# One of four VectorE softmax patterns made by an accumulating DMA, with 560 instead of 504 score tiles on VectorE

## The chip, the core and the metric

The kernel runs on one core of one Trainium2 chip. The metric is device time in microseconds (us); the kernel before has a median of 757.29 us in three runs. Engines are named as the profile names them: PE is TensorE (matrix products; PEld its weight loads), ACT is ScalarE, DVE is VectorE, POOL is GpSimd, SP is the engine that issues most DMAs.

## The reference, cut to what matters

```
x = A_x                                   # 2048 tokens x 512, 32 heads of 16
g = sigmoid((x * gate_w).sum(-1))         # a gate for each token
qkv = x @ A_wqkv
p = softmax(q @ k.T * 16 ** -0.5)         # per head, 2048 x 2048 scores
a = (p @ v) @ A_wo
# branch B: linear attention over the same x
phi_q = [softmax(q' @ w_phi), softmax(-q' @ w_phi)], phi_k likewise
b = (phi_q @ (phi_k.T @ v') / den) @ B_wo
return g * a + (1 - g) * b
```

Nearly all the work is the softmax attention of branch A: 32 heads with 2048 x 2048 scores each, every one of which has to go through an exponential.

## The kernel before, in words

**Tiles.** A unit is a score tile of 128 keys x 512 queries of one head. There are 2048 of them, in 512 rows ("packs") of four heads; sixteen rows make a group g (all keys of four heads against one chunk of 512 queries), so there are 32 groups. Scores are computed transposed (keys on partitions), on one of four strips of 32 rows of the PE array (`_scores`, L1040). The product with the values (`_values`, L1147) runs on one of four strips of 32 columns and adds up in a PSUM bank that stays open for the group. A column of ones in the values gives the denominator, and `_norm` divides at the group's end.

**Two ways to an exponential.** Most units go to ACT, two at a time: `_exp` (L1088) reads 128 x 1024 scores from PSUM and writes bf16 into `ET`, a ring of `NSLOT` = 22 tiles. The exponential of tile a waits for the value product of tile a - `NSLOT`. The units in `away` go to DVE: `NUMS` says how many in each of the 32 groups, 504 in all. DVE makes the exponential out of bits. `v_bits` (L946) scales a score and adds an origin, rounds to a 16-bit whole number, and those bits are read as a bf16 number, a piecewise linear 2^x. To smooth the error, four such patterns are made, with the bits shifted by 0, 31, 64 and 95; the last two are multiplied with values scaled by `RATIO` (`V2`), and all four products add up in the same accumulator (`pvx`).

**A batch** (`_vector_batch`) is four such units. Before, DVE writes the first pattern into the first half of a tile `va` (two buffers), one step instruction (L971) makes the second pattern beside it (2048 elements, + 31), and one step of 4096 elements makes patterns three and four from both in a tile `vs` (two buffers, + 64). So all four patterns are in memory side by side, and each has its own four matmuls.

**The order of the work** is written out by a planner (`Plan`) when the program is built. Every instruction is an `Op` with an engine, an assumed cost, a priority (roughly the row at which it is due) and the Ops that it depends on. `order` repeatedly takes the Op that could start earliest by these costs; among those ready it goes by `rank`. `now` is the row of the latest scores. An Op with `urgent` at or below `now` goes ahead. `shift` adds a pseudo-random offset to the priorities, drawn from `SEEDS`, once ahead of the ordering. The result is a fixed queue for each engine; `emit` puts a semaphore wait where an Op needs another engine's result. An engine carries out its queue strictly in this order, POOL and SP with their DMA issues among them. `o.port` marks POOL's instructions and some of DVE's, the steps among them, which the planner doesn't lay over one another.

**PSUM** has eight banks: four (`NRING`) hold scores for ACT, the others serve the accumulators, DVE's scores, the projections and branch B. **Fills:** where PE would have little to do, the planner puts matmuls with zeros into the open accumulator (`_fill`, L1154).

**Other lines that matter here.** Projections of q, k and v (L711, L827), the masks of q on POOL (L803), values scaled for `V2` on POOL (L844), the transposition of an accumulator on DVE (L1168), its normalisation on DVE and POOL (L1176 to L1185) and the small DMAs that regroup it (L1191). Branch B's maxima, sums and reciprocals run on DVE and POOL, its exponentials on ACT (L1335, 16 of them). `LEAD` = 7 says how many rows ahead of its first unit a batch's scores are due, `QDUE` = 20 how many rows ahead a q projection is, and `URGENT` = 4 how many rows after its own a value product becomes urgent.

Of the kernel before, what the change touches and what calls it, by code (L numbers as in the profile page):

```python
# [7 lines left out]
ALU = mybir.AluOpType  # L8
AX = mybir.AxisListType

P = 128
# [28 lines left out]
class Op:  # L40
    def __init__(self, eng, fn, cost, name, prio, rel, kind, lat):
# [21 lines left out]
        self.group = None  # L63


class Plan:
# [11 lines left out]
    def __init__(self):  # L78
# [11 lines left out]
        self.todo = {}  # L90

# [18 lines left out]
    def op(self, eng, fn, cost, reads=(), writes=(), deps=(), name="", prio=0.0, rel=-99, kind="full",  # L110
# [23 lines left out]
        o.port = eng == "POOL" or eng == "DVE" and name in self.PORT  # L134
# [5 lines left out]
    SEEDS = (3340, 7601, 0, 849, 2310, 7659, 5600, 4117, 3297, 4434, 5571, 2308, 3491, 696, 0, 2037, 1043, 4583, 3197, 9690, 0, 1465, 7801, 8165, 7230, 6142, 5708, 481, 3824, 4801, 1237, 3959, 2876, 7231)  # L140

    def shift(self):
        count = {}
        for o in self.ops:
            k = count[o.name] = count.get(o.name, 0) + 1
            s = self.SEEDS[min(max(int(o.prio // 16), 0), 33)] if o.prio >= 0 else 0
            if s:
                h = sum(map(ord, o.name)) * 7919 + k * 104729 + s * 65537
                h = (h ^ h >> 13) * 2654435761 & 0xFFFFFFFF
                o.prio += (s % 3 + 1) * (((h ^ h >> 16) & 1023) / 511.5 - 1)  # L150
# [64 lines left out]
    def order(self):  # L215
        avail = {e: [] for e in self.ENGS}
        for o in self.ops:
            o.left = len(o.deps)
            for d in o.deps:
                d.users.append(o)  # L220
# [9 lines left out]
        while left:  # L230
            best = None
# [94 lines left out]
    def emit(self, nc, ctx):  # L326
# [6 lines left out]
        count = dict.fromkeys(self.ENGS, 0)  # L333
        for e, q in self.queues.items():
            for o in q:
                if o.name.startswith("dma"):
                    o.sem = (ctx.enter_context(nc.semaphore(o.name)), 16 * len(o.fn) if isinstance(o.fn, list) else 16)
# [70 lines left out]
class _Kernel:  # L408
    NRING = 4
    GROUPS = (2, 2)  # L410
    NSLOT = 22
# [4 lines left out]
    NA, NST, LEAD = 2, 2, 7  # L416
# [21 lines left out]
    ALONE, EARLY = 12, 10  # L438
    PVP = 10
# [18 lines left out]
    def build(self):  # L458
        with ExitStack() as ctx:
# [10 lines left out]
            p.shift()  # L470
# [4 lines left out]
    def _memory(self, ctx):  # L475
# [67 lines left out]
        tiles = [sb(f"vs{k}", [P, 2, self.PACK, QCH], U16) for k in range(self.NST + self.NA)]  # L543
        self.vs, self.va = tiles[:self.NST], tiles[self.NST:]
# [341 lines left out]
    NUMS = (6, 10, 16, 14, 14, 16, 16, 19, 13, 19, 17, 12, 17, 11, 19, 19, 14, 20, 12, 16, 19, 13, 17, 16, 15, 20, 12, 20, 17, 21, 21, 13)  # L886

    def _plan_vector(self):
# [13 lines left out]
        self.hooks = {}  # L902
# [17 lines left out]
    def _vector_batch(self, number, units, due):  # L920
# [10 lines left out]
        for j, u in enumerate(units):  # L931
# [16 lines left out]
            if j < 2 * pairs and j % 2:  # L948
# [4 lines left out]
                def two(e, j=j, jobs=twin[j // 2]):  # L953
                    lo, hi = sorted(x.bank for x in jobs)
                    return bits(e, va[:, 0, j - 1:j + 1, :], self.ps[:, lo:hi + 1:hi - lo, :])
                parts.append(op("DVE", two, self.c_dve(1024), deps=[first[0], m] + war, name="v_bits", prio=first[2],
                                release=first[1], also=job))
            else:
                parts.append(op("DVE", lambda e, j=j, job=job: bits(e, va[:, 0, j, :], self._bank(job)),
# [4 lines left out]
        slot = self.n_step % self.NST  # L964
        self.n_step += 1
        vs, b_vs, b_vb = self.vs[slot], self.b_vs[slot], self.b_vb[number % self.NA]
        for k in range(4):
            tile, buf = (vs if k > 1 else va)[:, k % 2], b_vs if k > 1 else b_vb if k else b_va
            if k in (1, 2):
                src, dst = (va[:, 0, 0:n], va[:, 1, 0:n]) if k == 1 else (va[:, :, 0:n], vs[:, :, 0:n])  # L970
                o = op("DVE", lambda e, k=k, src=src, dst=dst: e.tensor_scalar(dst, src, float(STEPS[k - 1]), None,  # L971
                                                                               op0=ALU.add),
                       0.16 + k * n * QCH * 0.00026, reads=[b_va] + [b_vb] * (k - 1), writes=[buf], name="v_step",
                       prio=units[0] / 4 - 4)
# [724 lines left out]
```

## Time and profile before

| what | us |
|---|---|
| runs, median (lowest to highest of 3) | 757.29 (757.25 to 759.3) |
| span of the profiled execution, first to last instruction | 755.8 |
| PE busy | 744.3 |
| DVE busy | 719.9 |
| ACT busy | 741.1 |
| POOL busy | 228.6 |

The profiled execution's own time is given only as its span; the runs' median lies 1.5 us above it. "Busy" is the time in which at least one instruction's record is open. On this core records of one engine overlap: the next instruction starts before the record of the one before has ended. So the pace of an unbroken run (start to start) is shorter than the mean length of a record, and both are used below. A line of a group reads: source line, engine, operation, out<-in, sizes, count, then busy us and mean ns of one, then the idle time of the engine just before these instructions and whom it waited for. A line of the timeline reads: start, length, engine, line, operation, count, and in brackets the idle time before it.

### The profile page before, as it was taken

The page shows a single profiled execution, that of the slowest core. Times are in us where ns is not written, and L with a number is a line of the kernel's source. Part 1 is how long each engine was busy: PE and PEld are TensorE (multiplying, and loading weights), DVE is VectorE, ACT ScalarE, POOL GpSimd, SP SyncE. Part 2 cuts the span into 40 slices and gives each one's busy share as a digit, 9 for nine tenths or more (in the row PEclk, how much of TensorE's full clock was granted, in tenths as well). Part 3 has the DMA queues.
Part 4 walks back from the last instruction along what each step waited for, and adds up shares of the span by engine and source line. Part 5 has one row for each costly group of instructions (what it writes and reads, how often), then busy time and mean ns, then how long its engine had stood idle before and what let it go on. Part 6 is the DMA issues. An engine that isn't in the chain of part 4 may idle for free.

```text
span 755.8 us, 17204 instructions
## 1 busy us (share of the span) xinstructions
PE 744.3 (98%) x7246; PEld 219.7 (29%) x7246; DVE 719.9 (95%) x1128; ACT 741.1 (98%) x796; POOL 228.6 (30%) x317
## 2 busy tenths in 40 slices
PE   8999999999999999999999999999999999999998
PEld 3323222323332222222232323222232222223222
DVE  4788999999999999999999999999999999999997
ACT  6999999999999999999999999999999999999996
POOL 2213206241534334234407051431615051260010
PEclk9999999999999999999999999999999999999999
DMA  9610000001001000000200312112022103111010
GB/s 220 144 24 6 9 8 6 12 2 15 2 2 15 1 8 10 6 11 3 42 15 19 40 24 48 30 34 39 8 47 33 29 23 44 22 30 28 2 15 29
DMA packets 89181, 20.79 MB, mean 28 GB/s; under 512 B 83472, under 2 KB 88592, under 8 KB 89104
## 3 DMA queue, kind: packets, MB, share of 16 engines
q1 hardware_dynamic: 87232, 18.92, 13.8%
q8 instruction: 56, 0.92, 0.5%
q10 hardware_dynamic: 1872, 0.79, 0.4%
q14 instruction: 21, 0.17, 0.1%
HBM read 4.21 MB, written 2.10 MB: 8 GB/s over the span
## 4 chain that ended last, share of the span: by engine, by line
ACT 69%; PE 18%; DVE 11%; DMA 1%; issue 0%
ACT ET L1088 67%; PE ps L1147 6%; PE ps L1040 6%; DVE vs L946 4%; PE ps L711 4%; DVE vs L971 3%; ACT bq L1335 3%; PE ps L1154 1%; DMA xT<-in_A_x_dram 1%; DVE bq L1332 1%; DVE onB L1500 1%; DVE T L1168 0%; DVE rinvB L1483 0%; DVE btree L1329 0%; DVE btree L1327 0%
## 5 line engine op out<-in xcount | busy, mean ns | idle before, releaser
L1088 ACT ACTIVATE ET<-ps 128x1024 bf16<-128x1024 f32 (+1 forms) x774 | 713.4, 1158 | 1.9 <-PE ps L1040 1.5
L946 DVE TENSOR_SCALAR vs<-ps 128x512 uint16<-128x512 f32 x504 | 323.5, 678 | 12.0 <-PE ps L1040 10.1
L1040 PE MATMUL ps<-qT,kT 32*128 32x512 bf16 (+1 forms) x2052 | 307.3, 384 | 4.1 <-ACT ET L1088 2.0
L971 DVE TENSOR_SCALAR vs<-vs 128x2048 uint16<-128x2048 uint16 (+1 forms) x252 | 241.8, 973 | 1.3 <-PE ps L1147 0.5
L1147 PE MATMUL ps<-vs,V 128*32 128x512 bf16 x2016 | 216.9, 384 | 1.1 <-DVE vs L971 0.7
L1147 PE MATMUL ps<-ET,V 128*32 128x512 bf16 x1544 | 193.8, 387 | 0.4 <-DVE vs L946 0.2
L1040 PEld LDWEIGHTS ps<-qT,kT 32*128 32x128 bf16 x2052 | 76.4, 91 | 300.4 <-ACT ET L1088 287.5
L1339 POOL TENSOR_TENSOR btree<-btree 128x512 f16<-128x512 f16 (+1 forms) x32 | 35.7, 1117 | 208.0 <-DVE btree L1337 207.0
L1147 PEld LDWEIGHTS ps<-ET,V 128*32 128x32 bf16 x1544 | 48.6, 94 | 81.3 <-issue 72.2
L1147 PEld LDWEIGHTS ps<-vs,V 128*32 128x32 bf16 x2016 | 50.1, 95 | 49.9 <-issue 28.0
L711 PE MATMUL ps<-WB,xT 128*128 128x512 bf16 x192 | 58.6, 384 | 0.0
L1154 PE MATMUL ps<-kT,zero 128*32 128x512 bf16 x604 | 58.4, 385 | 0.0
L1324 POOL TENSOR_SCALAR bq<-bq 128x1024 bf16<-128x1024 bf16 x16 | 20.2, 1262 | 105.8 <-DVE bq L1306 64.9
L803 POOL TENSOR_SCALAR qT<-qtmp,mask 128x512 bf16<-128x512 bf16 x30 | 26.7, 897 | 55.6 <-DVE qtmp L798 51.0
L711 PE MATMUL ps<-xT,WA 128*128 128x512 bf16 x120 | 37.1, 384 | 0.3 <-DVE onB L1500 0.3
L1185 POOL TENSOR_TENSOR T<-T,rinv 128x512 bf16<-128x512 f32 x15 | 19.6, 1305 | 55.1 <-DVE rinv L1183 54.9
L1335 ACT ACTIVATE bq<-bq 128x2048 bf16<-128x2048 bf16 x16 | 32.8, 2047 | 0.0
L1168 DVE STREAM_TRANSPOSE T<-ps 128x512 f32<-128x512 f32 x32 | 22.6, 706 | 4.5 <-PE ps L1147 4.4
L1306 DVE CAST bq<-ps 128x512 bf16<-128x512 f32 x32 | 21.6, 679 | 0.7 <-PE ps L711 0.6
L844 POOL TENSOR_SCALAR V<-V 128x544 bf16<-128x544 bf16 x16 | 10.7, 670 | 36.0 <-DVE V L837 35.7
L711 PEld LDWEIGHTS ps<-WB,xT 128*128 128x128 bf16 x192 | 13.1, 97 | 24.8 <-issue 20.5
L1332 DVE TENSOR_TENSOR bq<-bq,btree 128x2048 bf16<-128x2048 bf16 x16 | 19.8, 1240 | 0.0
(91 smaller groups left out, 420.9 us busy)
## 6 DMA issues: line engine op xcount, KB each, us to landing
T<-T SPq DMA_DIRECT2D x240, 8.0 KB, 1.8
WB<-in_B_wqkv_dram SPq DMA_DIRECT2D x1, 1536.0 KB, 8.6
out_dram<-WB SPq DMA_DIRECT2D x12, 128.0 KB, 1.7
WA<-in_A_wqkv_dram SPq DMA_DIRECT2D x2, 384.0 KB, 5.3
WoB<-in_B_wo_dram SPq DMA_DIRECT2D x1, 512.0 KB, 3.9
WoA<-in_A_wo_dram SPq DMA_DIRECT2D x1, 512.0 KB, 4.8
WA<-in_A_wqkv_dram ACTq DMA_DIRECT2D x2, 128.0 KB, 3.3
WA<-in_A_wqkv_dram ACTq DMA_DIRECT2D x1, 256.0 KB, 4.9
```

Of the source, the lines that this page charges most:

```text
L711: return e.matmul(out, lhs, rhs, start=start, stop=stop)
L803: x = self.plan.op("POOL", lambda e, side=side: e.tensor_scalar(self.qT[:, s0 + side, :], tmp, self.mask[:, side:side + 1], 0.0, op0=ALU.m ...
L946: bits = lambda e, to, src: e.tensor_scalar(to, src, SCALE * LOG2E * 128.0, float(ORIGIN), op0=ALU.mult, op1=ALU.add)
L971: o = op("DVE", lambda e, k=k, src=src, dst=dst: e.tensor_scalar(dst, src, float(STEPS[k - 1]), None, op0=ALU.add), 0.16 + k * n * QCH * 0 ...
L1040: return e.matmul(out[:, cols], self.kT[32 * i:32 * i + 32, cp, kt * TOK:(kt + 1) * TOK], self.qT[32 * i:32 * i + 32, s, cols], start=True ...
L1088: o = plan.op("ACT", lambda e: e.activation(self.ET[:, a % NS:a % NS + n, cols], self.ps[:, a % NR:a % NR + n, cols], ACT.Exp, scale=SCALE ...
L1147: ins = e.matmul(self._bank(ot)[32 * i:32 * i + 32, :], v[:, v0:v0 + 32], tile, start=(kt == 0), stop=(kt == self.NT - 1), tile_position=( ...
L1154: ins = e.matmul(self._bank(ot)[32 * i:32 * i + 32, :], self.zero[:], self.kT[:, 0, 0:QCH], start=False, stop=False, tile_position=(0, 32 ...
L1168: t1 = op("DVE", lambda e: e.transpose(T1[:, side].rearrange("p b s -> p (b s)"), src()), 0.735, deps=last, writes=[b_T1[side]], name="n_t ...
L1332: + [("b_sub", two(2048), lambda e: e.tensor_tensor(x, x, spread(tree[:, :, 0]), ALU.subtract))],
L1335: op("ACT", lambda e: e.activation(flat, flat, ACT.Exp), 1.789, reads=[b], writes=[b], name="b_exp", prio=due + 1)
L1339: + [("b_sum", two(128 * n), lambda e, n=n: e.tensor_tensor(half[:, :, 0:n], half[:, :, 0:n], half[:, :, n:2 * n], ALU.add), (n <= self.P_ ...
```

## The change

The four patterns become 0, +31, +95 and +64. DVE makes the first from the scores and the second and third from the first, each in an instruction of 2048 elements, into a tile `vb` of two halves (two buffers). The fourth takes the place of the first in `va`: once the first pattern's matmuls and both steps have read it, POOL issues a DMA that adds 64 to every element (`accum_op=ALU.add`, from a tile `steps` that holds 64 everywhere). So `va` is half as large, and there are five of it. The first four and the last two batches have the fourth pattern made by DVE (`PLAIN`, kind "V"). `ET` has 16 tiles instead of 22. DVE gets 560 units. The planner has a model of the additions (`C_ADD` for the issue, `FIRST`, `MOVES` and `LANDED` for the transfer; additions follow one another), and offsets the priorities anew every eight rows from a longer list of seeds. Additions of one buffer share a semaphore that counts up. A bank in which the last output tiles are summed up is no longer handed out.

The diff, cut to its core (the numbers in `SEEDS` are left out):

```diff
-    SEEDS = (3340, 7601, 0, 849, 2310, 7659, 5600, 4117, 3297, 4434, 5571, 2308, 3491, 696, 0, 2037, 1043, 4583, 3197, 9690, 0, 1465, 7801, 8165, 7230, 6142, 5708, 481, 3824, 4801, 1237, 3959, 2876, 7231)
+    EVERY = 8
+    FIRST, LANDED = 1.45, 0.4
     def shift(self):
+        if len(self.SEEDS) <= self.drawn or self.now < self.EVERY * self.drawn:
+            return
+        s = self.SEEDS[self.drawn]
+        self.drawn += 1
         for o in self.ops:
+            if o.start is None and o.base >= 0:
+                h = (o.code + s * 65537) & 0xFFFFFFFF
                 h = (h ^ h >> 13) * 2654435761 & 0xFFFFFFFF
+                o.prio = o.base + (s % 4 * (((h ^ h >> 16) & 1023) / 511.5 - 1) if s else 0.0)
...
-        o.port = eng == "POOL" or eng == "DVE" and name in self.PORT
+        o.port = eng == "POOL" and not name.startswith("dma") or eng == "DVE" and name in self.PORT
...
         while left:
+            self.shift()
...
                 port = o.end if o.port else port
+                if o.moves:
+                    self.chan = max(t + self.FIRST, self.chan) + o.moves
+                    o.lat = self.chan + self.LANDED - o.end
...
-    NSLOT = 22
+    NSLOT = 16
-    NA, NST, LEAD = 2, 2, 7
+    NA, NB, LEAD = 5, 2, 7
+    C_ADD, MOVES, ADD_AT, PVD = 0.9, 2.8, -1, 0
+    KINDS, PLAIN = "D", (4, 2)
+    def _kind(self, number):
+        return self.KINDS[number % len(self.KINDS)] if self.PLAIN[0] <= number < self.n_batch - self.PLAIN[1] else "V"
...
-    NUMS = (6, 10, 16, 14, 14, 16, 16, 19, 13, 19, 17, 12, 17, 11, 19, 19, 14, 20, 12, 16, 19, 13, 17, 16, 15, 20, 12, 20, 17, 21, 21, 13)
+    NUMS = (7, 14, 15, 20, 16, 16, 20, 16, 16, 17, 17, 18, 18, 18, 18, 16, 19, 19, 20, 19, 21, 18, 18, 20, 15, 19, 17, 17, 20, 20, 21, 15)
...
+        kind, vb, (b_v1, b_v3) = self._kind(number), self.vb[number % self.NB], self.b_vb[number % self.NB]
+        last = (vb[:, 0], b_v1) if kind == "E" else (vb[:, 1], b_v3)
+        tiles = [(va, b_va), (vb[:, 0], b_v1), last, (va, b_va)]
+        def make(dst, by, reads, writes, prio):
+            o = op("DVE", lambda e: e.tensor_scalar(dst[:, 0:n], va[:, 0:n], float(by), None, op0=ALU.add),
+                   0.16 + n * QCH * 0.00026, reads=reads, writes=writes, name="v_step", prio=prio)
+            o.urgent = units[0] // 4 - self.AHEAD + 2
+        def add(k, tile, buf):
+            o = self.dma("POOL", f"add{number}_{k}", lambda e: e.dma_start(tile[:, 0:n], self.steps[:, 0:n], accum_op=ALU.add),
+                         cost=self.C_ADD, reads=[self.b_steps], writes=[buf], prio=units[0] / 4 + self.ADD_AT)
+            o.stream, o.moves = f"dma_add{k}_{number % (self.NB if k == 2 else self.NA)}", self.MOVES * n / 4
+            o.urgent = units[0] // 4 - self.AHEAD + 4
+        make(vb[:, 0], STEPS[0], [b_va], [b_v1], units[0] / 4 - 4)
+        if kind != "E":
+            make(vb[:, 1], sum(STEPS), [b_va], [b_v3], units[0] / 4 - 4)
+        for k in (0, 1, 2, 3) if kind != "E" else (0, 1, 3, 2):
+            tile, buf = tiles[k]
+            if k == 3 and kind == "V":
+                make(va, STEPS[1], [], [b_va], units[0] / 4 - 1)
+            elif k == 3 or k == 2 and kind == "E":
+                add(k, tile, buf)
...
-                x = op("PE", run, 0.23, reads=[buf], deps=list(found.values()), name="pvx", prio=units[0] / 4 - 2,
+                x = op("PE", run, 0.23, reads=[buf], deps=list(found.values()), name="pvx", prio=units[0] / 4 - (self.PVD if k == 3 else 2),
...
+        self.plan.op("POOL", lambda e: e.memset(self.steps[:], STEPS[1]), 1.0, writes=[self.b_steps], name="steps", prio=-5)
```

More of the change, by code (lines that the diff above doesn't have):

```diff
@@ L63, in __init__ @@
         self.group = None
+        self.stream = None
+        self.moves = 0.0
+        self.base = prio
+        self.code = 0
 class Plan:
@@ L90, in __init__ @@
         self.todo = {}
+        self.drawn, self.chan = 0, 0.0
     def _pass(self, kind, strips, t, cost):
@@ L542, in _memory @@
         self.outt = self.WB[:, 0:2, 2 * D:3 * D]
-        tiles = [sb(f"vs{k}", [P, 2, self.PACK, QCH], U16) for k in range(self.NST + self.NA)]
-        self.vs, self.va = tiles[:self.NST], tiles[self.NST:]
+        self.va = [sb(f"va{k}", [P, self.PACK, QCH], U16) for k in range(self.NA)]
+        self.vb = [sb(f"vb{k}", [P, 2, self.PACK, QCH], U16) for k in range(self.NB)]
+        self.steps = sb("steps", [P, self.PACK, QCH], U16)
         self.sbuf_used = at[0]
@@ L963, in _vector_batch @@
         b_va.writers, b_va.readers = parts, []
[L964 to L974, printed above, removed]
-                o.urgent = units[0] // 4 - self.AHEAD + 2
+        kind, vb, (b_v1, b_v3) = self._kind(number), self.vb[number % self.NB], self.b_vb[number % self.NB]
@@ L1091, in _exp @@
         if a >= len(self.mine) - NR:
-            o.on_commit = lambda o: plan.free_banks.extend((x % NR, plan._seen(o, "PE"), [o]) for x in range(a, b))
+            o.on_commit = lambda o: plan.free_banks.extend((x % NR, plan._seen(o, "PE"), [o]) for x in range(a, b)
+                                                           if x % NR not in self.ringout)
         self.exps.append(o)
@@ L1623, in _out @@
                 job.bank = (self.bank2[1] + tt - 4 + self.RINGOUT) % self.NRING
+                self.ringout.append(job.bank)
             for x in first:
```

31 lines of the change are left out of this document (16 added, 15 removed).

## The prediction

> **What bounds the kernel now.** I read the busy times first, then the groups of instructions with shapes kept apart, the chain that ended last, and the busy time by stretch.
>
> ```profile
> span 755.8 us, 17204 instructions
> PE 744.3 (98%) x7246; PEld 219.7 (29%) x7246; DVE 719.9 (95%) x1128; ACT 741.1 (98%) x796; POOL 228.6 (30%) x317
> ```
>
> Three engines look full: ScalarE (ACT), TensorE (PE), VectorE (DVE). The groups tell them apart (after the bar: busy us, mean ns of one; then idle before them).
>
> ```profile
> L1088 ACT ACTIVATE ET<-ps 128x1024 bf16<-128x1024 f32 x770 | 711.2, 1160 | 1.2 <-PE ps L1040 0.9
> L946 DVE TENSOR_SCALAR vs<-ps 128x512 uint16<-128x512 f32 x504 | 323.5, 678 | 12.0 <-PE ps L1040 10.1
> L971 DVE TENSOR_SCALAR vs<-vs 128x4096 uint16<-128x4096 uint16 x126 | 154.9, 1233 | 0.8 <-PE ps L1147 0.5
> L971 DVE TENSOR_SCALAR vs<-vs 128x2048 uint16<-128x2048 uint16 x126 | 89.1, 713 | 0.5
> L1154 PE MATMUL ps<-kT,zero 128*32 128x512 bf16 x604 | 58.4, 385 | 0.0
> ```
>
> ACT's exponentials waited 1.2 us in all. PE spends 58.4 us on 604 fill matmuls that compute nothing, so its 98% holds a reserve. DVE waits for scores for 12.0 us.
>
> The chain (start, length, what):
>
> ```profile
> 12.24 54.18 ACT ET L1088 x59
> 75.72 36.67 ACT ET L1088 x40
> 560.88 49.50 ACT ET L1088 x54
> ```
>
> In unbroken stretches one exponential of two tiles takes 54.18/59 = 0.918 or 49.50/54 = 0.917 us, though a record lasts 1160 ns: records overlap, so work is counted by the pace and not by the length. One score tile thus costs ACT 0.459 us.
>
> Busy time by stretch:
>
> ```profile
> 0.00:25.00 25.00, 22.57 (x140) 8.79 (x143) 14.29 (x26) 17.92 (x23) 6.27 (x18) 1.00 1.05 229
> 25.00:50.00 25.00, 25.00 (x244) 8.08 (x237) 18.45 (x27) 25.00 (x29) 6.07 (x8) 1.00 0.17 47
> 50.00:75.00 25.00, 25.00 (x206) 8.17 (x204) 22.78 (x38) 25.00 (x27) 5.79 (x11) 1.00 0.10 22
> 200.00:300.00 100.00, 99.64 (x941) 29.87 (x939) 98.77 (x156) 100.00 (x108) 38.10 (x53) 1.00 0.05 7
> 500.00:600.00 100.00, 98.42 (x1049) 28.87 (x1053) 98.33 (x155) 99.92 (x108) 31.15 (x39) 1.00 0.20 30
> 730.00:756.00 26.00, 22.72 (x218) 6.90 (x216) 20.73 (x34) 18.51 (x21) 0.00 (x0) 1.00 0.10 27
> ```
>
> The columns after the length are PE, its loads, DVE, ACT, POOL, the clock (1.00 throughout), DMA share, GB/s. From 25 us to the tail ACT is at 100%: **ACT sets the time**, with DVE close behind (98 to 99%). DVE's idle lies in the first 75 us: 10.71 + 6.55 + 2.22 = 19.5 us.
>
> **The change part by part.**
>
> *Fewer tiles on ACT.* NUMS sums to 504 before and 560 after: 56 tiles, 28 exponentials fewer. At 0.917 that is **-25.7 us** on the engine that sets the time. It becomes span only if DVE, POOL, DMA and PE keep up.
>
> *DVE's work.* Its pace is again read from runs:
>
> ```profile
> 418.09 4.23 DVE L946 TENSOR_SCALAR vs<-ps 128x512 uint16<-128x512 f32 x7
> ...
> 556.93 0.69 DVE L971 TENSOR_SCALAR vs<-vs 128x2048 uint16<-128x2048 uint16 x1
> 557.53 1.22 DVE L1332 TENSOR_TENSOR bq<-bq,btree 128x2048 bf16<-128x2048 bf16 x1
> 558.66 1.22 DVE L971 TENSOR_SCALAR vs<-vs 128x4096 uint16<-128x4096 uint16 x1
> 559.80 0.24 DVE L1476 SCALAR_TENSOR_TENSOR rinvB<-ps,ghB,eps 128x32 f32<-128x32 f32 x1
> ```
>
> Seven first patterns take 4.23 us: (4.23 - 0.68)/6 = 0.592 each. A step of 2048 elements takes 557.53 - 556.93 = 0.60, one of 4096 takes 1.14. Before, a batch of four has steps of 0.60 + 1.14 = 1.74, and 126 batches 219.2 us. After, 560/4 = 140 batches: 134 with two steps of 2048 (1.20) and, by PLAIN, six with three (1.80): 160.8 + 10.8 = 171.6. Steps -47.6, first patterns 56 x 0.592 = +33.2: **DVE -14.4 us**, less than ACT's -25.7, so DVE's idle must shrink by 11.3.
>
> Where? NUMS puts 10 of the 56 tiles into the first four groups (46 to 56). There ACT loses 4.6 us and DVE gains 10 x 0.592 - 11.5 x 1.74 + 4 x 1.80 + 10 x 1.20 = +5.1, of its 19.5 idle: 9.8 stay. In the rest, 46 tiles: ACT -21.1; DVE 27.2 - 114.5 x 1.74 + 124 x 1.20 + 2 x 1.80 = -19.6. **Both shrink alike**, so the balance at which ACT was fed to 100% is kept. I take no cost here; if DVE's cover fails, every us that it is late is a us of the span.
>
> *PE.* Four pattern matmuls for each of 56 tiles more, one value matmul fewer: +168 column matmuls. At the fills' 58.4/604 that is 16 us, which 58.4 us of fills can give up. Nothing.
>
> *Ring of 16 instead of 22.* An exponential now needs the value product of 16 tiles before.
>
> ```profile
> 8.19 2.16 ACT L1088 ACTIVATE ET<-ps 128x512 bf16<-128x512 f32 x4 [0.66 <-PE ps L1040]
> 10.88 1.02 ACT L1088 ACTIVATE ET<-ps 128x1024 bf16<-128x1024 f32 x1 [0.53 <-PE ps L1040]
> 12.22 18.44 ACT L1088 ACTIVATE ET<-ps 128x1024 bf16<-128x1024 f32 x20 [0.32 <-PE ps L1040]
> ...
> 17.83 0.40 PE L1147 MATMUL ps<-ET,V 128*32 128x512 bf16 x4
> ```
>
> Four tiles come from the halves, two at 10.88, two each from 12.22 on: the 17th is due at 12.22 + 5 x 0.92 = 16.8, and the first value product ended at 18.2. The price is 0 (V projected earlier) to 1.4 us, once; nearest the rows is **+1.4**. Later the products follow within `URGENT` = 4 rows, some 12 tiles: nothing.
>
> *The additions.* 134 accumulating DMAs of 512 KB from POOL; no row shows one. Nearest (median us from issue to landing; then two issues each on SP):
>
> ```profile
> WB<-in_B_wqkv_dram SPq DMA_DIRECT2D x1, 1536.0 KB, 8.6
> WoB<-in_B_wo_dram SPq DMA_DIRECT2D x1, 512.0 KB, 3.9
> WoA<-in_A_wo_dram SPq DMA_DIRECT2D x1, 512.0 KB, 4.8
> q1 hardware_dynamic: 87232, 18.92, 13.8%
> ```
>
> ```profile
> 419.73 1.25 SPq L1191 DMA_DIRECT2D T<-T  x2
> 421.02 2.70 SPq L1451 DMA_TRANSPOSE phiT<-bq  x2
> ```
>
> One addition occupies the DMA engines for 8.6/3 = 2.9 us by the large load, up to 5.7 if reading the target as well as the source doubles it. A batch comes every 731/140 = 5.2 us; with today's 13.8% (0.7 us of each 5.2) there is room for 4.5. I take 2.9, as the nearest row moves bytes of this size; both ends stay for the range. Landing after 3.9 to 4.8 us is hidden: `va` has five buffers, so one comes up again after 26 us, and its use spans the seven rows of LEAD (10 us) plus the landing. Issue costs POOL 0.6 to 1.35 us: 80 to 181 on top of 228.6, so POOL is at 42 to 56%. The addition waits for the first pattern's matmuls and for both steps; behind it in POOL's order stand the q masks, the reciprocals and the normalisation. The masks are the ones the scores wait for; their projection is due QDUE = 20 rows (28 us) ahead, so a hold of some us is covered. The addition itself holds PE only at the fourth pattern, whose priority is put off to the batch's own row (PVD).
>
> *POOL against DVE.* Undisturbed steps lasted 0.69 and 1.22; the means are 713 and 1233 ns, 0.02 and 0.01 us more, so 228.6 us of POOL cost DVE at most 126 x 0.03 = 4 us. In proportion the additions' issue costs 1.5 to 3 us more, spread over DVE's idle; the bounds are 0 and 181 (each issue stops DVE throughout). I take the proportion, and nothing on the span. The Trainium skill ("SBUF — State Buffer", Who interferes with whom) says that a VectorE instruction in a two-port mode and GpSimd lock each other out for a whole instruction, descriptor writing included. By it an addition behind a step starts up to 0.6 us late, which changes nothing, and a step behind an addition waits for the issue, which is the first rival. The rows here bear it out only as far as those 0.01 to 0.02 us.
>
> *The rest.* New SEEDS, drawn again every 8 rows, give another order. What an order can win is small: ACT's idle is 755.8 - 741.1 = 14.7 us, of which 25 - 17.92 = 7.1 and 26 - 18.51 = 7.5 lie at the two ends. What it can lose is in the rivals. The one memset of `steps` on POOL falls into a stretch where POOL is busy 6.27 of 25 us; the semaphores shared by additions and the banks kept back for the last output tiles issue nothing. Nothing for all three.
>
> **Sum.** 755.8 - 25.7 + 1.4 = 731.5 of span. The median of the runs is 757.29, 1.5 above this execution's span, which I keep: **733.0 us**.
>
> **The rivals.**
>
> *Additions and steps exclude each other on DVE's side.* If a step that comes while POOL writes an addition waits for it, then with an issue of 0.9 (between 0.6 and 1.35) POOL is in additions 134 x 0.9/731 = 16% of the time; 286 steps x 0.16 x 0.45 = 21 us. DVE by records becomes 719.9 + 36.0 (56 x 323.5/504) - 41.8 (154.9 + 89.1 - 286 x 0.707) = 714.1, + 21 = 735, with the 10 us of start and end that it can't fill: 745, 747 as a median. For: DVE has little left. Against: means so close to the undisturbed.
>
> *The additions move too slowly: slower than before.* At 5.7 us each the DMA engines are the bound: 134 x 5.7 = 764, plus some 35 us ahead of the first and 20 behind the last: about 820 us. It decides from (757 - 55)/134 = 5.2 us an addition. For: reading the target doubles the bytes; SP's small transfers share the engines. Against: 2.9 by the large load, and 13.8% of those engines in use today.
>
> *The saved exponentials aren't the bound.* If the fourth pattern comes late, PE closes accumulators late and ACT loses what it saved: 752 to 760. Against: PE has fills to spare and closing has a whole group (23 us) before its bank is wanted again.
>
> **How the numbers follow.** Forecast 0.63 (its own range 728 to 739: the cut at 0.917 to 711.2/770 = 0.924 an exponential, ring 0 to 1.4, up to 6 us of DVE lateness); better than 726, by a tighter start and end, 0.04; steps excluded 0.16, 739 to 757; not the bound 0.06; slow additions 0.11. What a measurement of this kernel can tell from no change is about 0.3%, 2.3 us. Faster: 0.63 + 0.04 + 0.14 + 0.02 = 0.83; within: 0.01 + 0.02 = 0.03; slower: 0.11 + 0.01 + 0.02 = 0.14. The range leaves out the better case (0.04), the slow additions (0.11) and the upper ends of the other two (0.05): 726 to 754.
>
> **What would show it.** Right: about 742 full exponentials, ACT at 100% from 25 us on, DVE 97 to 98% busy with 286 steps of 2048 at 0.70 us, fewer fills, additions landing in under 6 us, 726 to 733 of span. Wrong: ACT waiting tens of us for scores, steps with means over 0.78 us, first patterns waiting for an addition or for matmuls on its tile, landings over 10 us.

## The result, and the profile after

The changed kernel takes 800.98 us (median of 4 runs, 798.26 to 806.49), the kernel before 757.37 beside it: a ratio of 1.058 (95%: 1.054 to 1.062), **43.6 us slower**, where 733.0 was forecast. The profiled execution took 800.84 us, its span is 799.0. Two of experiment 9's four runs (847.79 and 858.25 us) were slow ones with a lower granted clock, and its time is given without them.

The page of the changed kernel, the same rows as shown of before, with the row of the granted clock (tenths, 40 slices) and the shares of the chain that ended last:

```profile
span 799.0 us, 17151 instructions
PE 749.3 (94%) x7104; PEld 219.2 (27%) x7104; DVE 718.0 (90%) x1218; ACT 726.0 (91%) x768; POOL 325.9 (41%) x452
PEclk9999999999999999999999898999999999979989
PE 45%; DMA 23%; DVE 18%; ACT 8%; POOL 4%; issue 2%; POOLq 0%; DVEq 0%
```

ACT's busy time fell by 741.1 - 726.0 = 15.1 us, and its idle time rose from 755.8 - 741.1 = 14.7 to 799.0 - 726.0 = 73.0. Idle +58.3, busy -15.1: +43.2 of span. No engine but PE is above 91%, 23% of the chain that ended last is DMA, and only 8% ACT. That is the sign of a kernel bound by waits, not by an engine's work; so the groups come next, and whom each waited for. PE's 94% holds time at a lower clock: the mean granted clock was 0.972 (before 1.000), so an estimated (1 - 0.972) x 799.0 = 22 us of PE's work at full rate were lost to it.

```profile
L1126 ACT ACTIVATE ET<-ps 128x1024 bf16<-128x1024 f32 (+1 forms) x746 | 696.5, 1066 | 57.7 <-PE ps L1078 52.4
L973 DVE TENSOR_SCALAR va<-ps 128x512 uint16<-128x512 f32 x560 | 363.7, 679 | 45.8 <-PE ps L1078 44.0
L996 DVE TENSOR_SCALAR vb<-va 128x2048 uint16<-128x2048 uint16 x280 | 199.6, 729 | 5.5 <-PE ps L1186 5.1
L1186 PE MATMUL ps<-va,V 128*32 128x512 bf16 x1120 | 137.7, 394 | 24.8 <-DMA va<-steps 23.9
L1193 PE MATMUL ps<-kT,zero 128*32 128x512 bf16 x292 | 29.6, 395 | 0.0
```

ACT's exponentials waited 57.7 us (before 1.2), DVE's first patterns 45.8 (before 12.0), both for scores: PE's scores come late. PE itself waited 23.9 us for additions in front of the fourth pattern's matmuls, though their tiles come up again only five batches later. That is less than half of what ACT lost, so something else must add to it. The waits of ACT and PE that matter (engine, line, waited for: us in total, times, longest):

```profile
ACT ET L1126 <- PE ps L1078: 52.4, 61, 7.3
PE ps L1186 <- DMA va<-steps: 23.9, 30, 1.8
PE ps L738 <- DMA WT<-onB: 8.4, 2, 7.0
```

Two waits of PE, 8.4 us, end with a small transpose of branch B issued by SP, which the change didn't touch. The stretches show when this happens:

```profile
50.00:75.00 25.00, 25.00 (x237) 7.29 (x229) 22.75 (x43) 25.00 (x29) 4.07 (x4) 1.00 0.34 64
200.00:300.00 100.00, 98.03 (x945) 31.13 (x943) 95.29 (x163) 96.97 (x103) 50.91 (x70) 1.00 0.55 101
500.00:600.00 100.00, 94.30 (x962) 26.14 (x955) 91.03 (x153) 94.71 (x104) 33.44 (x43) 1.00 0.76 134
```

ACT is still full from 50 to 75 us, as before; it is at 97% from 200 to 300 and under 95% from 500 to 600, where DMA is busy for 0.76 of the time (before 0.20). How one late addition spreads: first the chain of these microseconds (start, length, what), then the timeline (start, length, engine, line, count, and in brackets the idle time before):

```profile
424.17 6.63 DMA va<-steps
...
430.84 3.49 PE ps L1186 x29
```

```profile
424.17 1.20 POOL L1001 DMA_DIRECT2D va<-steps  x1 [3.40 <-PE ps L1078]
...
430.84 0.62 PE L1186 MATMUL ps<-va,V 128*32 128x512 bf16 x4 [1.84 <-DMA va<-steps]
432.10 0.64 PE L1186 MATMUL ps<-va,V 128*32 128x512 bf16 x4
...
434.27 0.39 PE L1078 MATMUL ps<-qT,kT 32*128 32x512 bf16 x4
434.70 5.61 ACT L1126 ACTIVATE ET<-ps 128x1024 bf16<-128x1024 f32 x6 [2.98 <-PE ps L1078]
```

The addition issued at 424.17 lands at 430.80, and PE stands for the last 1.84 us of it. The scores that ACT wants next stand behind these matmuls in PE's fixed queue, and the 29 matmuls that come between run at about half the clock (the third number from the end: 1.00 before, 0.59 from 430 us on):

```profile
420.00:430.00 10.00, 8.47 (x88) 2.26 (x85) 9.79 (x18) 9.88 (x11) 3.52 (x4) 1.00 0.48 80
430.00:434.00 4.00, 3.16 (x29) 1.09 (x29) 1.89 (x3) 1.71 (x2) 1.48 (x2) 0.59 1.08 189
```

So PE's wait of 1.84 us comes with one of 2.98 us on ACT. And how a late transpose does, first SP's row, then PE's:

```profile
695.09 3.39 SPq L1548 DMA_TRANSPOSE WT<-onB  x1
```

```profile
705.43 1.04 PE L738 MATMUL ps<-WoB,WT 128*128 128x512 bf16 x2 [7.04 <-DMA WT<-onB]
```

The transpose was issued from 695.09 to 698.48; PE's matmuls that need it stood until 705.43. Over these 10.3 us the DMA share was 1.14 (it can pass 1, as a transfer's time is counted where it starts), though over the span the two large queues come to 62%: the engines are full here, and not on the mean.

### The profile page after: what moved, and what is told of

Same layout as the page of the kernel before. It is cut to its first block, busy times and chain, and to the rows that moved or that the text cites. A ratio compares the mean times of both kernels' runs of the same rounds, so it can differ in the third digit from the quotient of the medians.

```text
span 799.0 us, 17151 instructions
## 1 busy us (share of the span) xinstructions
PE 749.3 (94%) x7104; PEld 219.2 (27%) x7104; DVE 718.0 (90%) x1218; ACT 726.0 (91%) x768; POOL 325.9 (41%) x452
## 4 chain that ended last, share of the span: by engine, by line
PE 45%; DMA 23%; DVE 18%; ACT 8%; POOL 4%; issue 2%; POOLq 0%; DVEq 0%
DMA va<-steps 21%; PE ps L1186 17%; PE ps L1078 14%; PE ps L738 9%; ACT ET L1126 7%; DVE va L973 7%; DVE vb L996 5%; DMA WT<-onB 2%; PE ps L854 2%; POOL va L1001 2%; DVE bq L1371 1%; PE ps L1193 1%; PE ps L727 1%; DVE bq L1345 1%; DVE btree L1366 1%
## 5 line engine op out<-in xcount | busy, mean ns | idle before, releaser
L1126 ACT ACTIVATE ET<-ps 128x1024 bf16<-128x1024 f32 (+1 forms) x746 | 696.5, 1066 | 57.7 <-PE ps L1078 52.4
L973 DVE TENSOR_SCALAR va<-ps 128x512 uint16<-128x512 f32 x560 | 363.7, 679 | 45.8 <-PE ps L1078 44.0
L1001 POOL DMA_DIRECT2D va<-steps x134 | 128.1, 973 | 273.7 <-PE ps L1186 100.5
L996 DVE TENSOR_SCALAR vb<-va 128x2048 uint16<-128x2048 uint16 x280 | 199.6, 729 | 5.5 <-PE ps L1186 5.1
L1186 PE MATMUL ps<-va,V 128*32 128x512 bf16 x1120 | 137.7, 394 | 24.8 <-DMA va<-steps 23.9
L1186 PE MATMUL ps<-vb,V 128*32 128x512 bf16 x1120 | 141.7, 396 | 0.9 <-DVE vb L996 0.9
L1186 PEld LDWEIGHTS ps<-va,V 128*32 128x32 bf16 x1120 | 32.6, 95 | 60.4 <-DMA va<-steps 42.6
L1186 PEld LDWEIGHTS ps<-vb,V 128*32 128x32 bf16 x1120 | 31.9, 96 | 23.5 <-issue 13.2
L1193 PE MATMUL ps<-kT,zero 128*32 128x512 bf16 x292 | 29.6, 395 | 0.0
L738 PE MATMUL ps<-WoB,WT 128*128 128x512 bf16 x64 | 21.1, 406 | 8.4 <-DMA WT<-onB 8.4
```

Of the source, the lines that this page charges most:

```text
L738: return e.matmul(out, lhs, rhs, start=start, stop=stop)
L973: bits = lambda e, to, src: e.tensor_scalar(to, src, SCALE * LOG2E * 128.0, float(ORIGIN), op0=ALU.mult, op1=ALU.add)
L996: o = op("DVE", lambda e: e.tensor_scalar(dst[:, 0:n], va[:, 0:n], float(by), None, op0=ALU.add), 0.16 + n * QCH * 0.00026, reads=reads, w ...
L1001: o = self.dma("POOL", f"add{number}_{k}", lambda e: e.dma_start(tile[:, 0:n], self.steps[:, 0:n], accum_op=ALU.add), cost=self.C_ADD, rea ...
L1126: o = plan.op("ACT", lambda e: e.activation(self.ET[:, a % NS:a % NS + n, cols], self.ps[:, a % NR:a % NR + n, cols], ACT.Exp, scale=SCALE ...
L1186: ins = e.matmul(self._bank(ot)[32 * i:32 * i + 32, :], v[:, v0:v0 + 32], tile, start=(kt == 0), stop=(kt == self.NT - 1), tile_position=( ...
```

## The experiments

**The theory:** the additions' engine work fits, as forecast, but PE waits for each landing inside a fixed queue, and 512 KB in flight makes SP's small transfers land late, for which PE also waits. **The rivals:** POOL's issue locks out DVE's steps; the order or the ring of 16 is at fault, and not the additions at all; the additions exceed the DMA engines. Unless said otherwise each kernel keeps every queue of the changed kernel in its order.

**1. PE does not wait for the additions.**

```diff
+            if o.name == "pvx":                # the wait moves to the tile's next writer
+                for a in [d for d in o.deps if d.name.startswith("dma_add")]:
+                    o.deps.remove(a)
+                    for u in o.users:
+                        if u.name == "v_bits":
+                            u.deps.append(a)
...
-    {u % 4: tile[:, place(j), :].bitcast(BF16)}
+    {u % 4: self.kT[:, 0, 0:QCH] if k == 3 and kind == "D" else tile[:, place(j), :].bitcast(BF16)}
```

> The changed kernel with the same five instruction queues, but the fourth pattern's matmuls read a tile of keys instead of the added tile and do not wait for the addition (the fourth pattern is left out of the result). The 134 additions of 512 KB are issued and land as before; only the next writer of the tile waits for them. Theory A (PE's fixed queue stands still at the fourth patterns because additions land after the moment that the order was made for, and the scores for ScalarE stand behind them): the time falls by most of what was lost, to 730 to 745 us, ACT's wait for scores from 52 us to under 12, the clock back to 1.00. Theory B (the additions' transfers and their issue on POOL slow DVE and the other DMAs): it stays at 790 to 805. Theory C (the order holds nowhere on the chip, whichever wait is taken away): it stays above 770.

Measured: 779.68 us (778.6 to 784.84), ratio 1.030 (1.027 to 1.034): **-21.3 us**. The waits of this kernel:

```profile
ACT ET L1133 <- PE ps L1085: 32.5, 33, 5.3
PE ps L745 <- DMA WT<-onB: 11.0, 4, 4.0
```

PE's wait for the added tile costs about half of the loss; ACT still waits 32.5 us, and now branch B's transposes stand at the top of PE's waits for DMA. Theory A expected 730 to 745 us and a clock back at 1.00; the time stayed above 770, which the expectation gave to theory C, and the clock at 0.971. So this wait alone is not the loss, and experiment 2 has to tell C from the rest.

**2. Small additions, all waits kept.**

```diff
-    e.dma_start(tile[:, 0:n], self.steps[:, 0:n], accum_op=ALU.add)
+    e.dma_start(tile[:, 0, 0:128], self.steps[:, 0, 0:128], accum_op=ALU.add)
```

> The changed kernel with the same queues and all its waits, but each addition adds to 128 elements of a partition instead of 2048 (32 KB instead of 512 KB; most of the fourth pattern is left out of the result). Theory A: landing falls from 5.6 us to about 2.5, under the planned 4.65, so PE's waits for additions vanish: 730 to 745 us. Theory B, if the transfers are what slows the others: the same; if it is the issue on POOL, 790 or more. Theory C: above 770.

Measured: 754.13 us (753.17 to 755.04), ratio 0.995 (0.994 to 0.997): **-46.9 us** with 134 issues and 134 waits in place.

```profile
ACT ET L1126 <- PE ps L1078: 13.7, 18, 4.0
```

With nearly all the bytes gone, nearly all the loss is gone, and the waits themselves cost almost nothing (1.2 us, by experiment 3). It is below theory C's 770 and misses the 730 to 745 of the others by 9 us.

**3. Both edits.**

> Both edits at once: small additions, and the fourth pattern's matmuls neither read nor await them. Against the run without the wait alone it prices the 512 KB transfers beside everything else: theory A expects under 5 us between the two, theory B 30 us or more.

Measured: 752.91 us (752.68 to 754.1), ratio 0.994 (0.993 to 0.996), 1.2 us below experiment 2. Against experiment 1 it differs only in the size of transfers that PE doesn't wait for, and those cost **26.8 us** (779.68 - 752.91). That is near theory B's 30, not theory A's 5. So full additions delay something other than the fourth pattern. SP's transposes are the first candidates: in experiment 1 PE waited 12.2 us for them, in experiments 2 and 3 the profile shows no such wait. The landing (us from the start of the issue) of those of branch B's output, before, after, and in this experiment (in experiment 1 it was 2.4/3.9/7.5):

```profile
DMA to landing us min/median/max: 2.4/2.5/3.9
```

```profile
DMA to landing us min/median/max: 2.4/3.1/10.3
```

```profile
DMA to landing us min/median/max: 2.4/2.5/4.4
```

**4. No addition issued, nobody waits; the fourth pattern is left out.**

```diff
+        self.queues["POOL"] = [o for o in self.queues["POOL"] if not o.name.startswith("dma_add")]
+        for o in self.ops:
+            o.deps = [d for d in o.deps if not d.name.startswith("dma_add")]
```

> The changed kernel's order without the additions: POOL doesn't issue them and nobody waits for them (the fourth pattern is left out of the result; its matmuls read keys). With small additions that nobody waits for, the time was 752.9 us, 20 above what the order was made for, and two steps of DVE took 2.1 and 3.0 us while POOL worked through a dense row of instructions, additions among them. Theory D (the issue of additions on POOL keeps DVE's steps from SBUF, and the scores wait for a bank that DVE frees late): 733 to 742 us, no step over 1.8 us, the clock at 1.00. Theory E (ring of 16, 560 tiles or the new order cost it, additions or not): 748 to 753.

Measured: 741.67 us (741.57 to 742.0), ratio 0.979 (0.977 to 0.980), **-11.2 us** against experiment 3, the clock at full speed throughout. That is what theory D expected (733 to 742, no step over 1.8 us), and not theory E. The same order and ring of 16 without the additions are thus 16.1 us faster than the kernel before beside it (757.77), so order and ring by themselves can be worth at most the 8.7 us that are left to the forecast. Its busy times:

```profile
PE 715.0 (97%) x7031; PEld 216.1 (29%) x7104; DVE 706.7 (96%) x1218; ACT 717.8 (97%) x768; POOL 210.1 (28%) x318
```

What POOL's issue does to DVE shows in the steps' durations (ns, min/median/max), in experiment 3, whose transfers are nearly empty, and here:

```profile
L1003 DVE TENSOR_SCALAR vb<-va x280: 624/684/2992, 26.5 to 738.8; 128x2048 uint16<-128x2048 uint16 x140
```

```profile
L1003 DVE TENSOR_SCALAR vb<-va x280: 622/681/1545, 26.2 to 727.7; 128x2048 uint16<-128x2048 uint16 x140
```

The median is nearly the same, the longest twice as long. One such place in experiment 3, DVE and POOL over the same stretch:

```profile
390.79 0.87 POOL L1008 DMA_DIRECT2D va<-steps  x1 [0.86 <-DVE vb L1003]
...
391.40 0.96 POOL L1385 TENSOR_TENSOR btree<-btree 128x256 f16<-128x256 f16 x1
...
391.61 3.73 DVE L1003 TENSOR_SCALAR vb<-va 128x2048 uint16<-128x2048 uint16 x2
392.06 0.97 POOL L837 TENSOR_SCALAR qT<-qtmp,mask 128x512 bf16<-128x512 bf16 x1
392.72 0.67 POOL L1388 TENSOR_TENSOR bsum<-btree 128x128 f32<-128x128 f16 x1
393.10 0.95 POOL L837 TENSOR_SCALAR qT<-qtmp,mask 128x512 bf16<-128x512 bf16 x1
394.13 0.66 POOL L1438 TENSOR_SCALAR guess<-bsum 128x128 uint16<-128x128 uint16 x1
```

Two steps take 3.73 us instead of some 1.3 while POOL works without a break: a step that meets such a row of POOL's instructions outlasts several of them. Two such places make up most of the 11.2 us: in experiment 3, 4.3 us of ACT's waits for scores end between 396 and 400 us and 5.2 between 446 and 455, with a mean clock of 0.68 from 440 to 456; here all of ACT's waits for those scores come to 3.5 us. An addition also holds back what stands behind it in POOL's queue. Whether its issue or the rows in which POOL then catches up delay the steps was not told apart.

**5. As 1, and PE doesn't wait for branch B's transposes either.** They are issued and land as before; PE's matmuls read keys instead.

```diff
+            if o.eng == "PE":
+                o.deps = [d for d in o.deps if not d.name.startswith(("dma_phit", "dma_ontb"))]
-    self.phiT[:, gg, ...], self.onTB[:, pr, ...]
+    self.kT[:, gg % 4, ...], self.kT[:, pr, ...]
```

> Full additions of 512 KB that PE doesn't wait for (as in the run without that wait, 779.7 us), and besides, PE no longer waits for the transposing DMAs of branch B on SP's queue: their matmuls read keys instead (branch B's result is left out), the DMAs are issued and land as before. Theory B2 (the additions' transfers cost time only because SP's transposes land later and PE's queue stands at the matmuls that need them): 752 to 760 us. If the transfers slow something else, the compute engines' access to SBUF for one: 770 or more.

Measured: 769.17 us (765.14 to 776.33), ratio 1.018 (1.012 to 1.025): **-10.5 us** against experiment 1. The theory expected 752 to 760, its rival 770 or more: the result misses the theory and lies just under the rival's. The four runs are 11 us apart, so this step is known to some 6 us only. 16.3 us above experiment 3 remain. In this kernel's profile PE still waits 3.0 us for a transpose of branch A's output and DVE 2.8 for its regrouping.

**6. As 5, and nobody but SP waits for any of SP's transfers after the loads.** The regrouping of branch A's output and the transposes read keys, so no tile waits for them, and their users read keys.

```diff
-            if o.eng == "PE":
-                o.deps = [... ("dma_phit", "dma_ontb") ...]
+            if o.eng != "SP":
+                o.deps = [d for d in o.deps if not d.name.startswith(("dma_phit", "dma_ontb", "dma_mix", "dma_back"))]
```

> The changed kernel's queues with full additions, but nobody other than SP waits for any of SP's transfers after the loads: the fourth pattern's matmuls, branch B's transposes and the regrouping of branch A's output are still issued and still take their place on the DMA engines, but they read a tile of keys, and their users on TensorE, VectorE, ScalarE and GpSimd read a tile of keys or their own sources without waiting. Left out: the fourth pattern, branch B's and branch A's true inputs of the last products. Theory (what is left of the additions' cost once the matmuls don't wait for them is the late landing of SP's small transfers): as with small additions, 751 to 757, ACT's waits for scores under 14 us. Rival (the remaining 16 us between 769.2 and 752.9 come from the additions in another way, such as a slower issue on POOL or VectorE's access to SBUF): 764 to 770, ACT's waits for scores 17 to 20 us.

Measured: 757.93 us (755.27 to 762.58, 10 runs), ratio 1.002 (0.999 to 1.004): a further **-11.2 us**. It lies 0.9 us above what the theory gave and far from the rival's 764. The two steps together, 21.7 us, are firmer than the border between them. With the small additions of experiments 2 and 3 the profile shows no wait for SP's transfers after the loads, so what the two steps save is a cost of the bytes, and not one that these waits have anyway. And all 134 full additions fit into 757.9 us, so the DMA engines are no bound that keeps the time at 800.

```profile
ACT ET L1136 <- PE ps L1088: 14.7, 22, 3.1
```

ACT's wait is back at 14.7 us, near experiment 2's 13.7, though not under the 14 expected. With full additions on the DMA engines, but nobody waiting for them or for SP, 757.93 - 752.91 = 5.0 us are left that I can't assign.

**7 and 8. Full additions in one part of the run only**, small ones in the other, all waits kept: the first 58 full (up to row 240), or the last 76.

```diff
+    x[:, 0:n] if units[0] < 960 else x[:, 0, 0:128]     # 7;   8: units[0] >= 960
```

> The changed kernel with its order and all waits, but additions from row 240 of 512 on are small (128 elements of a partition instead of 2048; that part of the fourth pattern is left out of the result). The 58 full additions lie before branch B's second stage, so no transposing DMA of its stage that PE waits for shares the engines with them. Theory B2 (the transposes that land late behind the additions make up the larger part): little over the 754 us of all small additions, 755 to 766. If what counts is PE's wait for the additions alone, which are spread evenly: 754 + 47 x 58/134 = 774.

> The reverse: the 58 additions before row 240 are small, the 76 after it full. Theory B2: 785 to 800. PE's wait for the additions alone: 754 + 47 x 76/134 = 781 or less. The two runs' excess over 754 should add up to the 47 us of the changed kernel if the two halves don't touch each other.

Measured: 760.6 us (758.27 to 768.09), ratio 1.005 (1.002 to 1.008), and 788.13 (785.95 to 795.53), ratio 1.042 (1.037 to 1.047). Above experiment 2 that is 6.5 us for 58 additions, 0.11 each, and 34.0 for 76, 0.45 each; together 40.5 of the 46.9. An addition of the same size costs four times as much in the part in which branch B's queries and outputs go through SP. Both times lie in the theory's ranges. But the transposes are not all of the difference: PE's waits for the additions themselves come to 7.3 us in 7 and 14.5 in 8, beside 9.6 for the transposes of branch B's output in 8 and none in 7. So experiments 5 and 6 carry the proof.

**9. A miss: the fourth pattern's matmuls later in PE's queue.** The whole computation; 147 groups moved behind the next one or two score instructions.

```diff
+        for x in [o for o in q if o.name == "pvx" and any(d.name.startswith("dma_add") for d in o.deps)]:
+            to = [i for i in range(at + 1, len(q)) if q[i].name.startswith("qk")][n - 1:n]
+            q.remove(x); q.insert(to[0], x)
```

> The whole computation, with the changed kernel's order but for one thing: each fourth pattern's group of matmuls is moved in PE's queue behind the next two instructions that make scores for ScalarE, or behind one where two would close a circle of waits (214 places in all for 147 groups, 1.5 on average, some 1.3 us). Theory A: most waits for additions become shorter by 0.9 to 1.8 us, PE's total wait for them falls from 66 us to under 30, the time to 755 to 780. Theory B: unchanged, 795 to 805. Theory C: unchanged or worse.

Measured: 830.8 us (826.95 and 834.67), ratio 1.097 (1.091 to 1.103), 30 us above the change itself, where theory A expected 755 to 780.

```profile
PE ps L1219 <- DMA va<-steps: 1.2, 2, 0.7
ACT ET L1159 <- PE ps L1111: 73.5, 145, 3.4
L1111 PE MATMUL ps<-qT,kT 32*128 32x512 bf16 (+1 forms) x2052 | 350.3, 395 | 11.1 <-DVE T L1240 6.6 <-DVE va L1006 1.3 <-DVE rinvB L1548 0.6
```

The waits for additions went (23.9 to 1.2 us), as intended. But the moved groups stand alone between score instructions, and the scores, 300.0 us of PE before the move, take 350.3. That standing alone makes them dearer is an inference from these two numbers. This repair of PE's queue by hand costs more than it saves: where matmuls stand side by side seems to matter as well as when.

**10 and 11. Two misses: the order planned anew with measured durations.** The planner's model had 4.65 us (median) from the start of an issue to landing and used the tile 0.48 us later (median). Here it gets the measured landings, SP's later ones, and POOL's issue as excluding DVE's steps; new seeds; 560 tiles, and 522.

```diff
-    FIRST, LANDED = 1.45, 0.4
+    FIRST, LANDED = 1.45, 1.2
-    C_ADD, MOVES, ADD_AT, PVD = 0.9, 2.8, -1, 0
+    C_ADD, MOVES, ADD_AT, PVD = 0.9, 3.2, -1, 0
-    lat=1.5 (mix), 1.7 (back), 2.3 (phit), 1.6 (ontb)
+    lat=2.0, 4.2, 3.3, 2.6
```

> The whole computation with 560 tiles and all 134 additions of 512 KB; only the planner's assumptions are changed to what the changed kernel's trace shows, and the order made anew with new seeds: an addition 0.4 us longer in transfer and 0.8 us later in landing, the transposes and regrouping DMAs on SP's queue 0.5 to 2.5 us later, and additions not laid over DVE's steps. The planner then ends at 777 us instead of 733. Theory A+B (what was lost was lost to durations that the order didn't allow for): the measured time lies within 1.5% of that, 777 to 790, below the 801 of the changed kernel though the plan is 44 us longer. Theory C (an order with additions doesn't hold on the chip, whatever it allows for): 20 us or more above its plan.

> The same assumptions with 522 tiles on DVE and 125 additions. The planner ends at 759 us. Theory A+B: 759 to 770 us, slower than the kernel before by up to 12 us: with orders found this far, honest durations leave nothing of the gain. Theory C: 780 or more.

Measured: 798.1 us (795.31 to 801.86), ratio 1.054 (1.050 to 1.058), and 793.96 (790.89 to 796.06), ratio 1.047 (1.045 to 1.050). The 560 tiles' waits, then the 522 tiles':

```profile
ACT ET L1126 <- PE ps L1186: 48.0, 7, 23.8
PE ps L738 <- DMA WT<-onB: 5.9, 1, 5.9
PE ps L1504 <- DMA phiT<-bq: 5.7, 1, 5.7
```

```profile
PE ps L1504 <- DMA phiT<-bq: 14.7, 2, 8.5
```

Both lie more than 20 us above their plans (20.6 and 35.3), as theory C expected and not theories A and B. The additions are waited for no more than 3.2 us in either. But with honest durations the planner's own timetables end at 777.5 and 758.7 (733.4 for the changed kernel, 753.2 for the one before, by the planner), so there is no gain left to lose; and the transposes' latest landings (13.6 and 11.9 us) exceed any allowance that I gave. PE's waits for these transposes come to 11.6 and 16.6 us; what else keeps the two above their plans is open. No version with full additions was found that beats the kernel before.

## Why the prediction was wrong

| what is taken away | us | step |
|---|---|---|
| nothing (the change) | 801.0 | |
| PE's wait for additions | 779.7 | -21.3 |
| PE's wait for branch B's transposes | 769.2 | -10.5 |
| all other waits for SP's transfers | 757.9 | -11.2 |
| the additions' bytes (SP's waits back in place) | 752.9 | -5.0 |
| the additions' issue | 741.7 | -11.2 |
| forecast | 733.0 | -8.7 |

**"Fewer tiles on ACT": right.** In the chain of the changed kernel, 21 exponentials in a row take 0.921 us each, so 28 fewer are worth 25.7, and without the additions (experiment 4) ACT's busy time is 741.1 - 717.8 = 23.3 us lower:

```profile
592.65 19.34 ACT ET L1126 x21
```

**"DVE's work": nearly right.** 286 steps; 718.0 us busy where the pace gave 719.9 - 14.4 = 705.5 and the records, in the first rival, 714.1. Without the issues it is 706.7, so the recipe of steps was right. With nearly empty additions (experiment 3) it is 713.4: the issues go with some 7 us of it, the rest was not split up.

**"PE, nothing" and the fills: right as far as work goes.** 604 fills became 292, and without the additions PE is busy for 715.0 us (before 744.3; 73 of its 7104 matmuls have no record there). That PE's clock could fall was not in the sum.

**"Ring of 16": +1.4, and then nothing: nearly right.** In the changed kernel ACT waits 1.42 us at the exponential that the prediction named, at 18.8 us, but later too:

```profile
ACT ET L1126 <- PE ps L1186: 3.6, 4, 1.4
```

**The additions' engine time: right.** 2.9 us each was taken; the queue's row gives 0.479 x 799.0/134 = 2.86.

```profile
q0 software_dynamic: 19296, 70.26, 47.9%
q1 hardware_dynamic: 87232, 18.92, 14.3%
```

The rival "the additions move too slowly" named 820 us, near the truth by its number alone: on the mean the engines were 62% busy, and full only in places.

**"Landing after 3.9 to 4.8 us is hidden: `va` has five buffers": the step that failed, 21.3 us.** I costed the landing by when the *buffer* is wanted again (26 us). It is wanted much sooner, by the fourth pattern's matmuls, and behind those stand scores in a queue that can't be rearranged. The landing itself was 5.6 us at the median and up to 11.2, over the 10 us that the prediction named as a sign of being wrong. The text said that the addition "holds PE only at the fourth pattern" and that this is put off to the batch's own row; it did not ask what stands behind. The rival "the saved exponentials aren't the bound" did have the fourth pattern coming late, but saw the harm in accumulators that close late, not in the scores behind, and priced it by the saving it would cancel (752 to 760). The landing of the additions in the changed kernel (us from the start of the issue):

```profile
DMA to landing us min/median/max: 4.5/5.6/11.2
```

**The DMA engines priced as throughput only: 21.7 us (10.5 + 11.2).** "There is room for 4.5" of each 5.2 us was right on the mean, and nothing was charged for it. Yet the additions come in clumps, as in the stretch with a DMA share of 1.14 above; a small transfer that meets one lands late, and its consumer stands in a fixed queue too. This cost stands nowhere in the prediction; the late landing of SP's transfers should have been a rival of its own.

**"POOL against DVE": 1.5 to 3 us in proportion, spread over DVE's idle, and nothing on the span: too small, 11.2 us.** The first rival feared that every step waits for an issue (21 us). What the trace shows is rarer and longer: steps have a mean of 729 ns, only 0.02 above the 0.707 that I used, but a few last through several of POOL's instructions, up to 2983 ns. In experiment 3 the granted clock drops after two such places. The Trainium skill's rule ("SBUF — State Buffer", Who interferes with whom) is that the loser fully blocks for a whole instruction; the trace agrees that a step stands still, but here one did so through several instructions in a row.

**The last 8.7 us: open in the main.** Without additions the kernel is still above 733.0. ACT's busy time there, 717.8, is 2.4 above 741.1 - 25.7, and its idle is 739.8 - 717.8 = 22.0 us against 14.7 before. Of that idle, 3.4 us are waits for value products, the ring's, where the sum had 1.4. For the rest, the start, the end, and the order fixed by durations that no longer hold are candidates; I tried none of them alone.

## What to carry to other kernels

A transfer is hidden only if what stands *behind its consumer* in that engine's queue can wait as well: ask for the next instruction in line, not for when the buffer comes up again. Moving bytes to DMA engines with room on the mean is not free for the small transfers already there, for they meet the clumps; a queue planned with latencies shorter than those that come breaks at its tightest waits. And when a planner sets the order, its assumed durations are terms of the prediction: check them against the nearest row, and see how much slack each leaves.

## What the runs showed of the hardware that I had not expected

- **TensorE's granted clock can halve after short stalls, but does not after each.** In the changed kernel's trace the clock is at 0.50 to 0.52 in eight stretches of 3.4, 6.8 or 10.2 us, 44 us together, and at 1.00 between them. Four begin beside a wait for an addition, of 1.28, 1.84, 1.19 and 1.23 us. Yet after waits of 1.65 us (at 507) and 1.28 us (at 641) the clock stayed at 1.00, so the length of the wait alone does not decide. The mean was 1.000 before, 0.972 after, and 1.000 without additions. The Trainium skill ("TensorE: Matmul & The Clock Gate", What's actually happening) gives half rate after an idle window of about 3.4 us; the stretches agree with multiples of that length, but here waits of half of it or less set one off. The rows after the wait at 194 us:

```profile
194.75 0.40 PE L1186 MATMUL ps<-va,V 128*32 128x512 bf16 x4 [1.28 <-DMA va<-steps]
195.09 0.58 PE L1078 MATMUL ps<-qT,kT 32*128 32x512 bf16 x4
...
198.50 0.41 PE L1078 MATMUL ps<-qT,kT 32*128 32x512 bf16 x2
```

- **An accumulating DMA inside SBUF** of 512 KB lands 4.5 us after the start of its issue at the earliest, one of 32 KB after 2.1. The Trainium skill ("DMA: Bandwidth & Descriptors", Anatomy of one DMA — SWDGE (gpsimd) path) fits a DMA on this path by 2.0 us and bytes at 436 GB/s, which would be an estimated 3.2 us here; the addition takes longer, and no run shows a plain copy of that size inside SBUF beside it. The issue costs POOL 883 ns at the median, and 883 for the small ones of experiment 2 too (the changed kernel's row):

```profile
L1001 POOL DMA_DIRECT2D va<-steps x134: 850/883/1577, 55.7 to 781.4; - x134
```

- **Small transfers land late though the engines are not full on the mean**: with 62% of the engines' time in use over the span, the latest transpose of branch B's output came after 10.3 us instead of 3.9. In just those 10.3 us the DMA share was 1.14 (before, from 700 to 712 us, 0.01), so what counts is the clump of additions that a transfer meets.
